# Sums of u squared of the last six chunks divided among three engines instead of two

## The chip, the core and the metric

The kernel runs on one core of one Trainium2 chip. The core has five engines that run side by side, each through its own queue in order: TensorE (PE, with PEld for its weight loads), VectorE (DVE), ScalarE (ACT), GpSimd (POOL) and SyncE (SP, which here only starts transfers). The metric is device time in microseconds. Three runs of the kernel before took 179.81, 180.15 and 180.93 us, so its median is 180.15 us.

## The reference

```python
kv = einsum('bhsd,bhse->bhde', k, v)     # per head: k^T v, 64 x 64
o  = q @ kv                            # 8 batches, 8 heads, 576 rows, 64 columns
x  = o / sqrt(mean(o*o, -1) + 1e-6) * g_norm       # then heads side by side: 4608 x 512
h  = x @ w_in                          # 4608 x 1024
e  = exp(h);   u = h * e               # softmax-weighted: solu = u / sum(e)
ln = (solu - mean(solu)) / sqrt(var(solu) + 1e-6) * g_ln
out = ln @ w_out                       # 4608 x 512
```

The kernel never forms `solu`. The factor 1/sum(e) cancels in the normalization apart from the 1e-6, so a row needs three sums over its 1024 columns: of e, of u and of u squared. They give one factor `rstd` per row, with which the product of u and the centred `w_out` is scaled.

## The kernel before

The 4608 rows are worked off in nine chunks of 512 (chunks 0 to 7 are 512 rows of a batch, chunk 8 gathers the last 64 rows of each batch). A chunk passes through: `kv_mm` (k^T v on PE, copied to `kvd`), `o_mm` (PE), `sq` (square of o, ACT), `s_mm` (mean over a head, PE), `ln` and `ex` (the root, ACT), `x` (DVE), the products with `w_in` (PE), exp (ACT), u (DVE), the turn of u, the products with `w_out` called `out` (PE), the scaling `ob` (DVE or ACT) and the `store` (SP).

Chunks 0 to 2 keep h with the 1024 columns on the partitions; their three sums are matmuls with a column of constants (`sums`), from squares `usq` and pair sums `es` that GpSimd makes. Chunks 3 to 8 (`TOK`) keep the rows on the partitions: `ht` makes 128 rows by 512 columns at a time, in eight pieces `ht.c.m.w` (m is one of four groups of 128 rows, w one of two column halves). `et` (exp) and `ut` (u) leave their row sums in `acc` by the accumulator of their instruction. The sum of u squared of a group, `st.c.m` (function `ht_sq`), is one instruction with an accumulator over 128x1024 elements, on ACT or DVE. `uT.c.y` turns u by a DMA transpose started on SP. `stats.c` (`rows_stats`, DVE) makes the variance from the 20 columns of `acc`, and `rstd.c` (ACT) its root.

The order of everything is written out ahead of time in the string `ORDER`: one entry for each piece, as `name@engine=slots`, with the engine where there is a choice and the numbers of the buffers that the piece takes (banks 0 to 7 of PSUM for matmul results, two slots `es` for the output of `st`, two slots for `u`, `acc` and others). The pieces are issued in this order, so it is the order of each engine's queue too. Whoever takes a buffer waits for its last users. Entries that matter here, with their meaning:

```
st.3.3@dve=1      sum of squares of rows 3 of chunk 3, on VectorE, output in es slot 1
ht.7.0.0=2        first product of chunk 7, into bank 2 (free when ut of the last product in it is done)
stats.5           variance of chunk 5: waits for all four st.5.m
```

Matmuls on zeros at the start (`warm`, 29 in all, their numbers in `WARM`) keep TensorE busy until data has come.

Of the kernel before, what the change touches and what calls it, by code (L numbers as in the profile page):

```python
# [20 lines left out]
warm.0=7 vf.0=00 ident kf.0=10 g q.0.0=0 v.0.1 k.0.1 q.0.1 vc.1@act q.1.0=1 vc.0@act k.1.0=1 kc.0@dve kc.1@act v.1.0=1  # L21
w_in.0 warm.1=7 qT_mm.0.0=0 w_in.1 kv_mm.0.0=1 qT.0.0@dve=0 kv.0.0.1@act kv.0.0.0@act k.1.1 kv.0.0.2@dve warm.2=7
o_mm.0.0=23 sq.0.0.0@act=00 sq.0.0.1@dve=11 warm.3=1 kv_mm.0.1=4 v.1.1 s_mm.0.0.0=5 kv.0.1.2@act turn_g=6 kv.0.1.1@dve
ex.0.0.0=0 g_mean qT_mm.0.1=7 q.1.1 s_mm.0.0.1=0 x.0.0.0=0 ex.0.0.1=1 qT.0.1@dve warm.4=5 qT_mm.1.0=1 w_out=01234567
kv.0.1.0@dve x.0.0.1 o_mm.0.1=56 sq.0.1.0@act=20 qT.1.0@dve=1 v.2.0=2 sq.0.1.1@act=31 warm.5=4 s_mm.0.1.0=2 ex.0.1.0=2
s_mm.0.1.1=0 kv_mm.1.0=7 k.2.0=2 ex.0.1.1=0 kv.1.0.2@dve table kv.1.0.1@dve kv.1.0.0@dve x.0.1.1 warm.6=2 o_mm.1.0=43
sq.1.0.1=0 x.0.1.0 warm.7=7 h_mm.0.0.0=1 sq.1.0.0=1 h_mm.0.4.0=2 s_mm.1.0.1=0 h_mm.0.2.0=7 ln.1.0.1=0 s_mm.1.0.0=6
h_mm.0.5.0=5 ln.1.0.0=1 h_mm.0.1.0=0 ex.1.0.0=1 h_mm.0.0.1 h_mm.0.7.0=6 ex.1.0.1=0 x.1.0.0=1 h_mm.0.1.1 exp.0.0=0
h_mm.0.7.1 x.1.0.1 h_mm.0.6.0=4 exp.0.1 u.0.0=0 h_mm.0.2.1 h_mm.0.6.1 usq.0.0@pool=0 u.0.1 exp.0.2=1 kv_mm.1.1=3
exp.0.6=2 u.0.2 h_mm.0.4.1 es.0.0=0 exp.0.7 kv.1.1.1@dve qT_mm.1.1=1 kv.1.1.0@dve exp.0.4=3 h_mm.0.5.1 qT.1.1@dve  # L30
# [5 lines left out]
h_mm.1.3.0=1 v.3.0=0 exp.1.6=2 h_mm.1.7.1 w_center.2 usq.0.4@pool exp.1.5 kv_mm.2.0=26 u.1.6 exp.1.7 h_mm.1.3.1
k.4.0=1 u.1.5 kv.2.0.2@act out.0.2.0=7 kv.2.0.1@act u.1.1 usq.0.7@pool kv.2.0.0@act kv.2.1.1@act qT_mm.2.0=3
w_center.7 kv.2.1.0@act kv.2.1.2@act qT_mm.2.1=2 es.1.0=1 qT.2.0@act=2 u.1.7 out.0.1.0=0 w_center.5 exp.1.3 v.4.0=1
o_mm.2.0=64 qT.2.1@dve out.0.3.0=3 sq.2.0.0=0 es.1.1 u.1.3 usq.1.0@act=1 s_mm.2.0.0=2 w_center.6 sums.0=1 ln.2.0.0=1
v.5.0=2 w_center.4 ex.2.0.0=0 es.1.3 o_mm.2.1=25 sq.2.0.1=1 turn.0 out.0.1.1 x.2.0.0=2 sq.2.1.0=2 usq.1.3@pool stats.0  # L40
out.0.3.1 sq.2.1.1=3 rstd.0 q_last.5 s_mm.2.1.0=6 s_mm.2.0.1=1 ob.0.3@dve=0 ln.2.1.0=0 out.0.2.1 usq.1.6@pool
ln.2.0.1=1 store.0.3 out.0.0.0=6 ex.2.1.0=2 usq.1.7@pool s_mm.2.1.1=3 ex.2.0.1=1 x.2.1.0 qT_mm.4.0=1 usq.1.5@pool
ln.2.1.1=0 out.0.0.1 ob.0.2@dve=3 ex.2.1.1=0 usq.1.1@pool x.2.0.1 qT_mm.3.1=2 qT_mm.3.0=3 x.2.1.1 kv_mm.3.0=74 q.7.0=2
qT.3.0@act=3 h_mm.2.0=5 usq.1.4@pool kv.3.1.1@dve qT.3.1@act ob.0.0@dve=1 h_mm.2.6=3 es.1.2 kv.3.1.0@dve ob.0.1@act=2
kv.3.0.2@dve qT.4.0@dve=0 h_mm.2.2=6 exp.2.0=0 q_last.2 kv.3.0.0@dve exp.2.6=3 u.2.0=0 h_mm.2.7=2 v.7.0=0 exp.2.2=2
u.2.6 h_mm.2.4=0 usq.1.2@pool exp.2.7 u.2.2 h_mm.2.3=1 kv.3.0.1@dve exp.2.4=1 k.5.0=2 u.2.7 h_mm.2.1=5 q_last.4
exp.2.3 u.2.4 kv.3.1.2@dve kv_mm.4.0=36 usq.2.0@pool=0 exp.2.1 u.2.3 o_mm.3.1=72 u.2.1 kv.4.1.1@act o_mm.3.0=04
es.2.0=0 sq.3.1.1=0 sums.1=1 kv.4.0.1@dve sq.3.1.0=2 kv.4.0.2@dve kv.4.1.0@dve es.2.1 sq.3.0.1=1 kv.4.1.2@dve
h_mm.2.5=5 turn.1 sq.3.0.0=3 stats.1 out.1.1.0=6 usq.2.1@pool exp.2.5 kv.4.0.0@dve usq.2.4@act s_mm.3.1.0=1 u.2.5
out.1.0.0=3 es.2.3 rstd.1 s_mm.3.0.0=5 ln.3.1.0=1 out.1.1.1 usq.2.6@pool ln.3.0.0=0 s_mm.3.1.1=1 ob.1.1@dve=7  # L50
out.1.0.1 ex.3.0.0=2 usq.2.2@pool ln.3.1.1=0 x.3.0.0=0 out.1.2.0=5 q_last.1 ex.3.1.0=1 s_mm.3.0.1=6 k.6.0=0 out.1.2.1
ex.3.1.1=0 x.3.1.0 usq.2.3@act usq.2.5@pool out.1.3.0=1 ob.1.0@dve=5 ln.3.0.1=1 x.3.1.1 store.1.0 q.6.0=1 o_mm.4.0=07
ex.3.0.1=2 ht.3.0.0=3 ob.1.2@dve=6 usq.2.7@pool sq.4.0.0=2 x.3.0.1 store.1.2 ht.3.0.1=6 et.3.0.0=00 es.2.2 ht.3.3.0=2
sq.4.0.1=3 store.0.2 et.3.0.1 v.6.0=1 out.1.3.1 et.3.3.0=2 k.7.0=1 s_mm.4.0.0=5 ob.1.3@dve=4 ht.3.2.0=4 ln.4.0.0=0
ut.3.0.0=1 ht.3.1.0=1 ex.4.0.0=1 ut.3.0.1 et.3.2.0=3 ht.3.3.1=5 x.4.0.0=1 et.3.1.0=1 ht.3.2.1=3 ut.3.2.0 st.3.0@act=1
ht.3.1.1=6 ut.3.1.0 ut.3.3.0 qT_mm.4.1=0 et.3.1.1 sums.2=4 qT.4.1@dve q.5.0=0 et.3.2.1 ut.3.1.1 q_last.7 o_mm.4.1=12
et.3.3.1 turn.2 out.2.0.0=0 q_last.3 ut.3.2.1 sq.4.1.1=0 q_last.6 out.2.1.0=6 ut.3.3.1 sq.4.1.0=1 q_last.0
st.3.1@dve=1 s_mm.4.1.1=3 s_mm.4.1.0=5 ln.4.1.1=1 out.2.0.1 stats.2 ex.4.1.1=0 out.2.3.0=3 st.3.2@dve=0 ln.4.1.0=0
out.2.2.0=4 rstd.2 x.4.1.1 ex.4.1.0=2 s_mm.4.0.1=5 out.2.2.1 st.3.3@act=1 x.4.1.0 out.2.1.1 ob.2.2@dve=0 ln.4.0.1=1
out.2.3.1 ob.2.1@dve=5 ex.4.0.1=1 ht.4.0.0=2 x.4.0.1 kv_mm.5.0=14 et.4.0.0=01 stats.3 ht.4.3.0=5 ob.2.3@dve=6  # L60
kv.5.1.1@act qT.5=1 kv.5.1.0@act ut.4.0.0=0 rstd.3 ht.4.1.0=6 et.4.3.0=1 kv.5.0.2@dve ob.2.0@dve=3 ht.4.3.1=7
et.4.1.0=3 kv.5.1.2@dve ht.4.2.0=3 ut.4.3.0 kv.5.0.0@act uT.3.0=1 et.4.3.1 ut.4.1.0 ht.4.1.1=2 et.4.2.0=2 kv.5.0.1@dve
ut.4.3.1 ht.4.0.1=0 et.4.1.1 ut.4.2.0 ht.4.2.1=4 store.2.1 et.4.0.1 ut.4.1.1 o_mm.5.1=56 et.4.2.1 ut.4.0.1 o_mm.5.0=17
kv_mm.7.0=32 sq.5.0.1=2 ut.4.2.1 uT.4.0=0 sq.5.0.0=0 s_mm.5.0.1=0 kv.7.0.1@dve kv.7.0.2@dve sq.5.1.0=1 s_mm.5.0.0=4
kv.7.0.0@dve ln.5.0.0=0 kv.7.1.2@dve out.3.1.0=3 kv.7.1.0@dve sq.5.1.1=3 kv.7.1.1@dve store.0.0 s_mm.5.1.0=4
st.4.1@dve=0 out.3.0.0=2 ex.5.0.0=0 uT.3.1 ln.5.1.0=1 out.3.1.1 x.5.0.0=2 ln.5.0.1=0 st.4.3@dve=1 out.3.0.1 ex.5.1.0=2
ex.5.0.1=1 kv_mm.6.0=41 store.2.0 x.5.1.0 st.4.2@act=0 s_mm.5.1.1=0 ob.3.0@dve=5 ht.5.0.1=5 store.2.3 x.5.0.1
ln.5.1.1=1 ht.5.0.0=2 ob.3.1@act=1 st.4.0@dve=1 store.1.1 ex.5.1.1=0 ht.5.1.0=0 et.5.0.0=10 qT.6=2 x.5.1.1 ht.5.1.1=7
kv.6.1.1@act kv.6.0.0@dve et.5.1.0=3 ut.5.0.0=1 ht.5.2.0=3 stats.4 et.5.1.1 out.3.3.0=6 uT.4.1 ut.5.1.0 et.5.2.0=0
ht.5.3.0=2 ut.5.1.1 rstd.4 out.3.3.1 kv.6.1.0@dve kv.6.0.1@dve et.5.0.1 store.1.3 ht.5.3.1=0 ob.3.3@dve=3 kv.6.0.2@act  # L70
# [731 lines left out]
```

## Time and profile before

| | before |
|---|---|
| median of three runs | 180.15 us |
| the profiled execution, its own time | 179.54 us |
| its span, first to last instruction | 177.8 us |
| PE, DVE, ACT, POOL busy | 166.1, 136.7, 145.5, 63.3 us |
| mean granted TensorE clock | 0.995 |
| transfers | 36.01 MB, mean 203 GB/s |

The span lies 1.74 us below the execution's own time; that part is ahead of the first and behind the last instruction. Busy times add up the durations of an engine's instructions; matmuls are pipelined, one shows 379 ns, but the next starts 0.216 us after it.

### The profile page before, as it was taken

The numbers are of one execution on the slowest core, as the hardware profiler recorded it, in microseconds if no ns is written. First come the engines' busy times: TensorE is split into PE (matmuls) and PEld (weight loads), VectorE is DVE, ScalarE is ACT, GpSimd is POOL, SyncE is SP. The second block draws the span as 40 slices with busy tenths as digits, with TensorE's granted clock in tenths as the row PEclk, the third lists the DMA queues.
The fourth block names the chain that finished last, engine by engine and source line by source line (L and its number), as shares of the span: only waits on it lengthen the run. The fifth ranks groups of instructions, "written<-read, shape, count | busy, mean of one in ns | idle before, by whom it ended". The sixth has DMA issues, their size and how long they took to land.

```text
span 177.8 us, 4448 instructions
## 1 busy us (share of the span) xinstructions
PE 166.1 (93%) x1725; PEld 81.6 (46%) x1746; DVE 136.7 (77%) x321; ACT 145.5 (82%) x294; POOL 63.3 (36%) x77
## 2 busy tenths in 40 slices
PE   7696999999999999999998999999999999999980
...
POOL 8754027999999999725000000000000000000000
...
GB/s 196 202 203 210 209 290 350 209 206 208 209 222 218 198 206 122 199 249 208 180 161 180 182 214 202 187 203 204 204 173 204 151 171 128 200 203 210 202 210 218
DMA packets 57737, 36.01 MB, mean 203 GB/s; under 512 B 39148, under 2 KB 51188, under 8 KB 57716
## 3 DMA queue, kind: packets, MB, share of 16 engines
...
q8 instruction: 13, 0.21, 0.5%
q14 instruction: 8, 0.07, 0.1%
...
## 4 chain that ended last, share of the span: by engine, by line
PE 82%; DVE 5%; ACT 5%; DMA 4%; issue 2%; POOL 0%; POOLq 0%
PE out_ps L685 31%; PE ht_ps L557 23%; PE h_ps L492 11%; DMA q_sb<-in_q_dram 4%; PE kv_ps L354 4%; PE s_ps L417 3%; PE o_ps L399 3%; PE sum_ps L641 2%; PE qT_ps L374 2%; ACT rst_sb L425 1%; ACT osq_sb L409 1%; DVE u_sb L507 1%; DVE kvd L189 1%; ACT lss_sb L421 1%; PE mean_ps L670 1%
## 5 line engine op out<-in xcount | busy, mean ns | idle before, releaser
L557 PE MATMUL ht_ps<-w_in_sb,x_sb 128*128 128x512 bf16 x188 | 44.0, 379 | 0.2
L685 PE MATMUL out_ps<-w_out_sb,usq_sb 128*128 128x512 bf16 x177 | 42.8, 379 | 0.5 <-DVE kvd L189 0.2
L567 ACT ACTIVATE e_sb<-ht_ps,zero_t 128x512 f32<-128x512 f32 x48 | 32.7, 685 | 5.7 <-PE ht_ps L557 5.0
L575 DVE SCALAR_TENSOR_TENSOR u_sb<-ht_ps,e_sb 128x512 bf16<-128x512 f32 x48 | 31.4, 684 | 1.0 <-ACT e_sb L567 0.7
L439 DVE SCALAR_TENSOR_TENSOR x_sb<-o_ps,g_sb,rst_sb 128x512 bf16<-128x512 f32 x36 | 26.2, 744 | 7.7 <-ACT rst_sb L425 7.5
L557 PEld LDWEIGHTS <-x_sb 128*128 128x128 bf16 x192 | 18.6, 98 | 22.4 <-DVE x_sb L439 0.2
L685 PEld LDWEIGHTS <-usq_sb 128*128 128x128 bf16 x184 | 17.7, 98 | 21.9 <-issue 1.3
L702 DVE TENSOR_SCALAR rooms<-out_ps,rstd 128x512 f32<-128x512 f32 x27 | 20.1, 748 | 8.6 <-PE out_ps L685 7.3
L409 ACT ACTIVATE osq_sb<-o_ps,zero_t 128x512 bf16<-128x512 f32 x35 | 22.1, 684 | 3.1 <-PE o_ps L399 2.9
L421 ACT ACTIVATE lss_sb<-s_ps,eps_t 128x512 f32<-128x512 f32 x32 | 21.3, 685 | 3.4 <-PE s_ps L417 3.3
L685 PE MATMUL out_ps<-w_out_sb,u_sb 128*128 128x512 bf16 x94 | 22.9, 379 | 0.2 <-issue 0.2
L492 PE MATMUL h_ps<-x_sb,w_in_sb 128*128 128x512 bf16 x91 | 22.1, 379 | 0.7 <-issue 0.3
L425 ACT ACTIVATE rst_sb<-lss_sb,zero_t 128x512 f32<-128x512 f32 x32 | 22.4, 724 | 0.4
L518 POOL TENSOR_TENSOR usq_sb<-u_sb 128x512 bf16<-128x512 bf16 x18 | 18.7, 1046 | 7.4 <-DVE u_sb L507 7.2
L586 DVE SCALAR_TENSOR_TENSOR es_sb<-u_sb 128x1024 bf16<-128x1024 bf16 x17 | 20.6, 1216 | 0.0
L500 ACT ACTIVATE e_sb<-h_ps,zero_t 128x512 f32<-128x512 f32 x24 | 15.4, 689 | 1.4 <-PE h_ps L492 1.3
L507 DVE TENSOR_TENSOR u_sb<-h_ps,e_sb 128x512 bf16<-128x512 f32 x24 | 15.5, 682 | 0.5 <-ACT e_sb L500 0.4
L524 POOL TENSOR_TENSOR es_sb<-e_sb 128x512 bf16<-128x512 f32 x12 | 15.3, 1275 | 1.2 <-ACT e_sb L500 1.1
L685 PEld LDWEIGHTS <-u_sb 128*128 128x128 bf16 x96 | 9.0, 98 | 10.8 <-issue 0.6
L417 PE MATMUL s_ps<-osq_sb,head_mean 128*128 128x512 bf16 x36 | 13.0, 379 | 1.0 <-ACT osq_sb L409 0.9
L492 PEld LDWEIGHTS <-w_in_sb 128*128 128x128 bf16 x96 | 8.8, 98 | 10.7 <-issue 1.1
L189 DVE CAST kvd<-kv_ps 64x128 bf16<-64x128 f32 (+1 forms) x31 | 8.9, 287 | 3.2 <-PE kv_ps L354 2.2
...
## 6 DMA issues: line engine op xcount, KB each, us to landing
out_dram<-rooms SPq DMA_DIRECT2D x66, 128.0 KB, 2.5
...
q_sb<-in_q_dram POOLq DMA_DIRECT2D x6, 512.0 KB, 10.4
...
```

Source lines behind the costliest of these rows:

```text
L409: nc.scalar.activation(out=t[:, :], in_=o, func=AF.Square, bias=zero_t[:, :])
L421: nc.scalar.activation(out=t[:, :], in_=T["s", i][:, :], func=AF.Ln, bias=eps_t[:, :])
L425: nc.scalar.activation(out=t.rearrange("p a b c -> p (a b c)"), in_=T["lss", i][:, :], func=AF.Exp, scale=-0.5, bias=zero_t[:, :])
L439: nc.vector.scalar_tensor_tensor(out=dst, in0=T["o", c, hf, z][:, :, :, :], scalar=g_rep[:, :], in1=T["rst", (c, hf, z)][:, :, :, :], op0= ...
L492: nc.tensor.matmul(T["h", c, f][:, :], w_in_sb[:, dt, f * 128:(f + 1) * 128], T["x", c][:, dt, :], start=(dt == 0), stop=(dt == NP - 1),)
L518: of(engine).tensor_tensor(out=dst, in0=src, in1=src, op=MUL)
L557: nc.tensor.matmul(t[:, :], T["x", c][:, dt, 128 * m:128 * m + 128], w_in_sb[:, dt, 512 * w:512 * w + 512], start=(dt == 0), stop=(dt == N ...
L567: nc.scalar.activation(out=T["e", c, m][:, w, :], in_=T["ht", c, m, w][:, :], func=AF.Exp, bias=zero_t[:, :], accum_out=T["acc", c][:, 2 * ...
L575: nc.vector.scalar_tensor_tensor(out=T["u", c][:, m, 512 * w:512 * w + 512], in0=T["ht", c, m, w][:, :], scalar=1.0, in1=T["e", c, m][:, w ...
L586: nc.vector.scalar_tensor_tensor(out=t, in0=u, scalar=1.0, in1=u, op0=MUL, op1=MUL, accum_out=total)
L685: nc.tensor.matmul(T["out", c, m][:, :], u_rows(c, f, m), w_out_sb[:, f, :], start=(f == 0), stop=(f == NF - 1),)
L702: nc.vector.tensor_scalar_mul(out=dst, in0=src, scalar1=by)
```

## The change

For chunks 3 to 8 `st` gets a third engine to choose from, GpSimd. There a sum is not one instruction but eleven: the product u times u into an fp32 tile of 128x1024, then ten additions of the right half to the left half (512, 256, ... 1 columns), the last of them into the column of `acc`.

```diff
     def ht_sq(engine, c, m):
+        u, total = T["u", c][:, m, :], T["acc", c][:, 16 + m:17 + m]
+        if engine == "pool":
+            t = tile_of(("es", c, m), [128, d_ff], FP32)
+            nc.gpsimd.tensor_tensor(out=t[:, :], in0=u, in1=u, op=MUL)
+            w = d_ff // 2
+            while w:
+                dst = t[:, 0:w] if w > 1 else total
+                nc.gpsimd.tensor_tensor(out=dst, in0=t[:, 0:w], in1=t[:, w:2 * w], op=ADD)
+                w //= 2
+            return
         t = tile_of(("es", c, m), [128, 2, d_ff], BF16)[:, 0, :]
-        u, total = T["u", c][:, m, :], T["acc", c][:, 16 + m:17 + m]
...
-            plan.add(("st", c, m), "act|dve", lambda e, c=c, m=m: ht_sq(e, c, m), ...
+            plan.add(("st", c, m), "act|dve|pool", lambda e, c=c, m=m: ht_sq(e, c, m), ...
...
-    WARM = (12, 4, 3, 2, 1, 2, 3, 2)
+    WARM = (12, 4, 6, 7)
```

The whole table `ORDER` is another one. It holds the same pieces (but the 29 warm matmuls stand in four groups instead of eight) in another order and partly on other engines. The 24 sums of squares go from 17 on DVE and 7 on ACT to 9 on DVE, 1 on ACT and 14 on POOL:

```diff
-st.3.0@act=1 st.3.1@dve=1 st.3.2@dve=0 st.3.3@act=1 st.4.1@dve=0 st.4.3@dve=1 st.4.2@act=0 st.4.0@dve=1
-st.5.2@dve=0 st.5.1@dve=1 st.5.3@dve=0 st.5.0@dve=1 st.6.1@dve=0 st.6.3@dve=1 st.6.2@act=0 st.7.0@dve=1
-st.6.0@dve=0 st.7.1@dve=1 st.7.3@dve=0 st.7.2@dve=1 st.8.0@act=0 st.8.2@dve=1 st.8.1@act=0 st.8.3@act=1
+st.3.0@pool=1 st.3.2@dve=0 st.3.1@pool=0 st.4.0@pool=1 st.4.2@pool=0 st.3.3@dve=1 st.4.3@pool=1 st.5.0@pool=0
+st.4.1@dve=1 st.5.1@pool=0 st.5.2@pool=1 st.5.3@pool=0 st.6.0@dve=1 st.6.1@pool=0 st.6.2@pool=1 st.6.3@act=0
+st.7.1@dve=1 st.7.2@pool=0 st.7.3@dve=1 st.7.0@dve=1 st.8.0@pool=0 st.8.1@dve=1 st.8.3@pool=1 st.8.2@dve=0
```

The stretch of the new table around `stats.5`, in full:

```
...
out.5.3.0=4 et.6.3.0=3 x.7.1.0 ht.6.1.1=2 sq.7.0.1=3 ut.6.3.0 out.5.0.1 et.6.1.1 stats.5
s_mm.7.1.1=3 out.5.3.1 ut.6.1.1 ln.7.1.1=0 st.6.0@dve=1 st.6.1@pool=0 uT.6.0=0 s_mm.7.0.1=0 ht.7.0.0=2 ln.7.0.1=1
...
```

And around the third `o_mm`:

```
...
kv_mm.1.0=4 x.0.0.1 ex.0.1.0=1 kv.1.0.1@dve table kv.1.0.2@dve x.0.1.0 x.0.1.1 kv.1.0.0@act warm.3=7 o_mm.1.0=52 h_mm.0.2.0=7
...
```

More of the change, by code (lines that the diff above doesn't have):

```diff
@@ L20 @@
 ORDER = """
[L21 to L30, printed above, removed]
@@ L36 @@
[L36 to L45, printed above, removed]
@@ L46 @@
[L46 to L70, printed above, removed]
@@ L96 @@
-store.8.0@sp store.8.1@act ob.8.3.1@dve store.8.2@act store.8.3.1@sp
+warm.0=7 vf.0=00 ident kf.0=10 g q.0.0=0 v.0.1 k.0.1 q.0.1 vc.0@dve q.1.0=1 vc.1@dve k.1.0=1 kc.1@act kc.0@dve v.1.0=1
+w_in.0 warm.1=7 qT_mm.0.0=0 w_in.1 kv_mm.0.0=1 kv.0.0.1@dve kv.0.0.2@dve v.1.1 kv.0.0.0@dve qT.0.0@dve=0 warm.2=7
+o_mm.0.0=23 turn_g=4 sq.0.0.0@dve=00 sq.0.0.1@act=11 k.1.1 kv_mm.0.1=5 s_mm.0.0.1=6 kv.0.1.2@act g_mean qT_mm.0.1=7
+q.1.1 kv.0.1.1@dve qT.0.1@dve kv.0.1.0@act ex.0.0.1=0 w_out=01234567 o_mm.0.1=10 s_mm.0.0.0=4 sq.0.1.1@act=21
```

104 lines of the change are left out of this document (73 added, 31 removed).

## The prediction, on record before the changed kernel ran

> **What bounds the kernel now.** I read the page first (span, busy time, slices), then the busy time by stretch, then the chain that ended last.
>
> ```profile
> span 177.8 us, 4448 instructions
> ...
> PE 166.1 (93%) x1725; PEld 81.6 (46%) x1746; DVE 136.7 (77%) x321; ACT 145.5 (82%) x294; POOL 63.3 (36%) x77
> ...
> PE   7696999999999999999998999999999999999980
> ...
> POOL 8754027999999999725000000000000000000000
> ```
>
> ```profile
> 70.00:95.00 25.00, 24.84 (x272) 12.23 (x276) 20.96 (x57) 22.27 (x54) 7.97 (x10) 1.00 1.23 196
> 95.00:128.00 33.00, 32.05 (x321) 15.14 (x321) 30.82 (x71) 31.57 (x67) 0.00 (x0) 1.00 1.00 196
> 128.00:162.00 34.00, 33.79 (x215) 15.57 (x218) 31.50 (x78) 27.72 (x65) 0.00 (x0) 1.00 0.85 178
> 162.00:178.00 16.00, 10.74 (x57) 5.48 (x56) 4.79 (x16) 6.66 (x13) 0.00 (x0) 0.93 0.82 208
> ```
>
> ```profile
> PE 82%; DVE 5%; ACT 5%; DMA 4%; issue 2%; POOL 0%; POOLq 0%
> ```
>
> In the stretches the columns behind the length are busy PE, PEld, DVE, ACT and POOL, then the granted clock. PE is the bound: from 70 to 162 us it is idle for 0.16 + 0.95 + 0.21 = 1.3 us at full clock, and it holds 82% of the chain. DVE and ACT follow closely (30.8 and 31.6 of 33 us between 95 and 128). POOL, empty from about 82 us on, is on the chain nowhere. So relieving DVE and ACT can give back 1.3 us here at most, while a wait that reaches PE costs its full length.
>
> **What a sum costs on GpSimd.** It takes 14 of the 24 sums over. On the engines that lose them a sum is one instruction of 1.2 us:
>
> ```profile
> L586 DVE SCALAR_TENSOR_TENSOR es_sb<-u_sb 128x1024 bf16<-128x1024 bf16 x17 | 20.6, 1216 | 0.0
> ...
> L584 ACT ACTIVATE es_sb<-u_sb,zero_t 128x1024 bf16<-128x1024 bf16 x7 | 8.0, 1142 | 0.0
> ```
>
> DVE is rid of 8 x 1.22 = 9.8 us, ACT of 6 x 1.14 = 6.8 us; both are hidden behind PE, so this is worth the idle time named above and no more. On POOL it is eleven instructions, each of which waits for the one before to be complete. No row has the fp32 addition in place; the nearest are these (duration and mean of one behind the bar; in the second fence start, duration):
>
> ```profile
> L518 POOL TENSOR_TENSOR usq_sb<-u_sb 128x512 bf16<-128x512 bf16 x18 | 18.7, 1046 | 7.4 <-DVE u_sb L507 7.2
> ...
> L524 POOL TENSOR_TENSOR es_sb<-e_sb 128x512 bf16<-128x512 f32 x12 | 15.3, 1275 | 1.2 <-ACT e_sb L500 1.1
> ```
>
> ```profile
> 0.74 0.20 POOL masks.py:197 MEMSET ident<- 128x128 bf16 x1 [0.29 <-POOLq L786]
> 1.02 0.29 POOL masks.py:199 TENSOR_SCALAR_AFFINE_SELECT ident<-ident 128x128 bf16<-128x128 bf16 x1
> 1.27 0.10 POOL masks.py:197 MEMSET eye<- 9x9 f32 x1
> 1.44 0.19 POOL masks.py:199 TENSOR_SCALAR_AFFINE_SELECT eye<-eye 9x9 f32<-9x9 f32 x1
> ...
> 78.28 0.74 POOL L278 DMA_DIRECT2D q_sb<-in_q_dram  x1 [4.01 <-PE qT_ps L374]
> 79.47 2.97 POOL L302 DMA_DIRECT2D q_last<-in_q_dram  x4 [0.45 <-issue]
> ```
>
> The tiny write of 9 elements shows 0.10 us, and the select that needs it starts 0.17 us after it: a fixed 0.10 and 0.07 to the next dependent one. With that, fp32 costs (1275 - 100) / 512 = 2.29 ns an element and bf16 (1046 - 100) / 512 = 1.85. The product: 1024 x 1.85 ns + 0.10 + 0.07 = 2.06 us. The additions run over 1023 elements in all: 1023 x 2.29 ns = 2.34 us, and 10 x 0.17 = 1.7 us fixed, 4.04. One sum: 6.1 us, which I take, since these rows are an fp32 operand and a dependent pair. With the additions at the bf16 rate it is 1.89 + 1.7 + 2.06 = 5.6. With the 0.19 us of the small select as fixed part, 2.12 and 1.67 ns an element follow, and 2.6 + 2.17 + 1.97 = 6.7; with the product at that fp32 rate too, 7.2. Below stands 4.2: 2047 elements at 1046 / 512 = 2.04 ns and nothing fixed. 14 x 6.1 = 85 us fit into the rest of the run; what matters is when each must be done.
>
> The GPSIMD Engine Reference of the Trainium skill, section 3.1, gives 4497 ns for an fp32 addition of 2048 elements, 2.2 ns an element against 2.29 here; by that estimate the sum would be 0.1 us shorter, 6.0, and the forecast 0.7 us lower.
>
> **When it must be done.** The new table puts st.3.0 on POOL behind the load q.5.0 and three q_last. By the last two rows above, with three of four (0.74 each), POOL is free at 78.28 + 0.74 + 0.45 + 2.2 = 81.7. Between st.3.0 and st.4.0 PE has 48 matmuls of 512 columns and two `kv_mm`; between st.4.0 and stats.5 it has 19 `out` and 16 `ht` groups of 4 and 10 `s_mm`, 150 matmuls, one `kv_mm` and six `o_mm`. Prices, from the chain in order of time and the timeline (start, length):
>
> ```profile
> 88.08 0.71 PE kv_ps L354 x72
> ...
> 143.85 5.18 PE ht_ps L557 x24
> ```
>
> ```profile
> 94.86 0.63 PE L399 MATMUL o_ps<-qT_sb,kvd 64*64 64x256 bf16 x16
> ```
>
> 5.18 / 24 = 0.216 a matmul. First stretch: 10.4 + 1.4 = 11.8 us, so st.4.0 falls due at 93.5. Second: 32.4 + 0.7 + 1.9 = 35.0, with half of the 0.95 us of idle time of that stage 35.5; stats.5 stands at 129.0 and reaches its third instruction at 129.4:
>
> ```profile
> 128.17 0.16 DVE L599 TENSOR_REDUCE two<-acc_sb 128x8 f32<-128x16 f32 x1
> ...
> 128.57 0.16 DVE L605 SCALAR_TENSOR_TENSOR var<-sq,acc_sb 128x4 f32<-128x4 f32 x1
> ```
>
> That is the first one that reads the sums of squares, so there DVE waits for st.5.3. Between the two places POOL's queue holds seven sums in a row: st.4.0, 4.2, 4.3, 5.0, 5.1, 5.2, 5.3. They fit if one takes (129.4 - 93.5) / 7 = 5.13 us or less. At 6.1 the two sums before end at 81.7 + 12.2 = 93.9, and the seven at 93.9 + 42.7 = 136.6: 7.2 us late. Behind the waiting instruction stands ut.6.1.1; it frees bank 2, which ht.7.0.0 needs, and PE has only six matmuls (1.3 us, what DVE needs for the rest of stats.5 and ut.6.1.1) before it. So PE stands still for about the 7.2 us. The earlier waits of DVE, st.3.3 for st.4.0's slot and st.4.1 for st.4.3's, are parts of the same lateness and not added. After stats.5 the remaining five sums lie 6 to 13 us apart, and st.8.3 has `out` groups behind it to the end; I add nothing.
>
> **The start.** In the new table the copy kv.1.0.0, which the third `o_mm` needs, is on ACT behind the table load:
>
> ```profile
> 18.24 1.28 ACT L445 ACT_TABLE_LOAD   x1
> ...
> 19.17 0.41 PE L399 MATMUL o_ps<-qT_sb,kvd 64*64 64x256 bf16 x8 [0.24 <-DVE kvd L189]
> ```
>
> ```profile
> L187 ACT CAST kvd<-kv_ps 64x128 bf16<-64x128 f32 (+1 forms) x17 | 4.3, 261 | 3.8 <-PE kv_ps L354 3.6
> ```
>
> 18.24 + 1.28 + 0.26 for a copy, and 0.05 to pass on, is 19.8 instead of 19.17: 0.7 us later, at a place where PE has only warm matmuls (bounds: 0, if the table load comes early enough, to 1.3, its whole length). The remaining moves of loads, copies and scalings have the same counts and I price them at nothing; the cover is PE's own work, and if it is gone, each costs a copy of 0.3 or a scaling of 0.7 us. The load queue keeps its transfers.
>
> **The sum**, against the profiled execution's 179.54 us (the median is 180.15): + 7.2 for the wait at stats.5, + 0.7 at the start, - 0.95 for idle PE time between 95 and 128 that lighter DVE and ACT give back. That is 186.5 us.
>
> **The rivals.**
>
> *GpSimd is in time.* If a sum takes up to 5.13 us, nothing waits: 179.54 + 0.7 - 0.95 = 179.3, no change. For it: the lower bound of 4.2, and four independent squares in 4.04 us on POOL, so that fixed parts can overlap. Against it: here each step needs the one before.
>
> *Faster.* GpSimd is in time, the start is not later, PE's 1.3 us of idle time vanish, and the last store lands sooner. It is issued at 173.34 and the span ends 4.5 us later, where stores take 2.5 us at the median:
>
> ```profile
> out_dram<-rooms SPq DMA_DIRECT2D x66, 128.0 KB, 2.5
> ```
>
> ```profile
> 173.34 0.33 SPq L715 DMA_DIRECT2D out_dram<-rooms  x1
> ```
>
> With 1 us of these 2, 179.54 - 1.3 - 1.0 = 177.2. It decides as soon as a sum is below 5.13 us. Against it: the tail's stores are as many as before, and PE's work is the same.
>
> *VectorE and GpSimd hold each other up.* The nine sums left on DVE read u from SBUF twice while POOL is reading too. If one had to stand until the other's instruction is over, DVE would lose up to 2.06 us at each, about 9 us at half; it has 33 - 30.82 + 34 - 31.5 = 4.7 us free and gains 9.8, so most is hidden. But POOL would lose 1.22 us to each of the two DVE sums inside its chain (st.3.3, st.4.1): with 5.13 us a sum, 179.3 + 2.4 and some 0.8 on PE for unhidden waits, 182.5; on top of the forecast, 188.9. No run here shows such a pair: POOL's last arithmetic ends at 72.8 and DVE's first sum comes later.
>
> ```profile
> 71.51 1.27 POOL L524 TENSOR_TENSOR es_sb<-e_sb 128x512 bf16<-128x512 f32 x1
> ```
>
> The page SBUF — State Buffer of the Trainium skill, section "Who interferes with whom", states this rule: a DVE instruction with two SBUF inputs contends with a GpSimd instruction that reads SBUF, and the second fully blocks.
>
> **How the numbers follow.** Chances: the wait at stats.5 0.55, the holding up alone 0.07 (slower together 0.62), in time 0.22 (no change), faster 0.16. A measurement of this kernel can tell about 1% from no change, 178.3 to 182.0. The forecast's own range: at 5.6 us a sum the chain ends at 93.5 + 39.2 = 132.7, 3.3 late, 182.6; at 6.7 it ends at 95.1 + 46.9 = 142.0, 12.6 late, 191.9 (at 7.2 it would be 196.4). The whole range goes from 178.5, which takes in most of the case without change, to 192.
>
> **What would show it.** In the profile after: POOL's steps with some 6.1 us from one product to the next between 94 and 137 us and no gap; a wait of DVE at the variance of chunk 5, for POOL, of about 7 us, the longest of the run; directly behind it a hole in PE ahead of an `ht` matmul. Waits of DVE for POOL also ahead of st.3.3. The third `o_mm` near 19.8. The forecast is wrong if products follow each other at 5.1 us or less, or if DVE waits and PE does not.

## The result, and the profile after

The changed kernel took 203.07 us at the median (201.56 to 205.79, six runs) beside 179.98 us of the kernel before: ratio 1.1243 [1.1176, 1.131]. Two of the six runs lie more than 1.5% above the fastest and are left out of the ratio. The kernel is slower, as predicted, but by some 22 us instead of the 7.0 of the prediction's sum, and outside the predicted range. The profiled execution took 201.56 us, 22.0 more than that of before. The page first:

```profile
span 199.8 us, 4610 instructions
...
PE 172.1 (86%) x1746; PEld 82.7 (41%) x1746; DVE 136.3 (68%) x304; ACT 138.7 (69%) x282; POOL 154.8 (77%) x232
...
PE   7868999999999999999934999998069998999930
...
POOL 8751089999799994989889988988877989178910
PEclk9999999999999999999995899999657999999996
...
POOL 42%; PE 34%; issue 6%; DMA 5%; ACT 5%; DVE 3%; ACTq 0%; POOLq 0%; DVEq 0%
```

POOL, empty from 82 us on before, is busy in nearly every slice behind that, and it now holds 42% of the chain that ended last. PE has two notches, and a lower clock behind each. Busy time by stretch (columns as before):

```profile
95.00:128.00 33.00, 26.52 (x209) 11.66 (x208) 22.87 (x53) 23.88 (x51) 29.24 (x53) 0.90 0.87 166
128.00:162.00 34.00, 26.50 (x124) 11.14 (x121) 19.31 (x47) 21.49 (x49) 28.32 (x55) 0.85 0.62 122
```

PE idles 6.5 and 7.5 us where it idled 0.95 and 0.21. What a sum costs stands in the groups of POOL by shape (busy time and mean of one, then the idle time ahead of all of them):

```profile
L585 POOL TENSOR_TENSOR es_sb<-u_sb 128x1024 f32<-128x1024 bf16 x14 | 28.1, 2008 | 7.2 <-DVE u_sb L576 6.8 <-ACT es_sb L594 0.4
L589 POOL TENSOR_TENSOR es_sb<-es_sb 128x512 f32<-128x512 f32 x14 | 20.3, 1454 | 1.1
...
L589 POOL TENSOR_TENSOR es_sb<-es_sb 128x2 f32<-128x2 f32 x14 | 2.7, 194 | 1.1
L589 POOL TENSOR_TENSOR acc_sb<-es_sb 128x1 f32<-128x1 f32 x14 | 2.7, 193 | 1.1
```

and the products in the timeline of POOL (start, length), the first of the run and four in a row:

```profile
82.56 1.94 POOL L585 TENSOR_TENSOR es_sb<-u_sb 128x1024 f32<-128x1024 bf16 x1
...
117.63 1.89 POOL L585 TENSOR_TENSOR es_sb<-u_sb 128x1024 f32<-128x1024 bf16 x1
...
125.29 1.89 POOL L585 TENSOR_TENSOR es_sb<-u_sb 128x1024 f32<-128x1024 bf16 x1
...
131.95 1.89 POOL L585 TENSOR_TENSOR es_sb<-u_sb 128x1024 f32<-128x1024 bf16 x1
...
138.61 1.89 POOL L585 TENSOR_TENSOR es_sb<-u_sb 128x1024 f32<-128x1024 bf16 x1
```

From product to product it is 6.66 us (131.95 to 138.61), or 7.66 (117.63 to 125.29) where something comes between. An addition of one or two columns takes 0.19 us and 0.08 pass to the next one (1.1 us over 14). Now the ends of this, in the timelines of DVE and PE (the wait and its releaser in brackets):

```profile
103.54 2.89 DVE L596 SCALAR_TENSOR_TENSOR es_sb<-u_sb 128x1024 bf16<-128x1024 bf16 x1 [5.43 <-POOL acc_sb L589]
...
145.34 0.16 DVE L615 SCALAR_TENSOR_TENSOR var<-sq,acc_sb 128x4 f32<-128x4 f32 x1 [8.30 <-POOL acc_sb L589]
...
191.06 0.16 DVE L615 SCALAR_TENSOR_TENSOR var<-sq,acc_sb 128x4 f32<-128x4 f32 x1 [2.67 <-POOL acc_sb L589]
```

```profile
107.16 0.61 PE L418 MATMUL s_ps<-osq_sb,head_mean 128*128 128x512 bf16 x1 [5.72 <-DVE x_sb L440]
...
146.36 3.57 PE L558 MATMUL ht_ps<-w_in_sb,x_sb 128*128 128x512 bf16 x8 [7.50 <-DVE u_sb L576]
...
190.70 1.04 PE L704 MATMUL acc_ps<-w_out_sb,usq_sb 128*128 128x256 bf16 x8
```

st.3.3 waits 5.43 us and PE stands 5.72 us behind it; the variance of chunk 5 waits 8.30 us and PE stands 7.50 us, ahead of ht.7.0.0. The last matmuls of before, for comparison:

```profile
171.75 1.04 PE L694 MATMUL acc_ps<-w_out_sb,usq_sb 128*128 128x256 bf16 x8
```

So the 22.0 us between the two spans fall into three parts: 145.34 - 128.57 = 16.8 us up to the variance of chunk 5; from there to PE's end 46.4 us instead of 44.2, 2.2 more; and behind PE's end 8.1 us instead of 5.0, 3.1 more.

One thing more is seen in DVE's groups. The nine sums left there last 1784 ns on average instead of 1216; the one at 103.54 above lasts 2.89 us:

```profile
L596 DVE SCALAR_TENSOR_TENSOR es_sb<-u_sb 128x1024 bf16<-128x1024 bf16 x9 | 16.1, 1784 | 5.5 <-POOL acc_sb L589 5.4
```

### The profile page after: what moved, and what is told of

Same layout as the page of the kernel before. It is cut to its first block, busy times and chain, and to the rows that moved or that the text cites. A ratio compares the mean times of both kernels' runs of the same rounds, so it can differ in the third digit from the quotient of the medians.

```text
span 199.8 us, 4610 instructions
## 1 busy us (share of the span) xinstructions
PE 172.1 (86%) x1746; PEld 82.7 (41%) x1746; DVE 136.3 (68%) x304; ACT 138.7 (69%) x282; POOL 154.8 (77%) x232
## 4 chain that ended last, share of the span: by engine, by line
POOL 42%; PE 34%; issue 6%; DMA 5%; ACT 5%; DVE 3%; ACTq 0%; POOLq 0%; DVEq 0%
POOL es_sb L589 26%; POOL es_sb L585 11%; PE h_ps L493 10%; PE out_ps L695 9%; PE ht_ps L558 7%; DMA v_sb<-in_v_dram 5%; PE sum_ps L651 2%; PE s_ps L418 2%; DVE u_sb L576 2%; POOL q_sb L279 2%; PE kv_ps L355 1%; ACT e_sb L501 1%; PE qT_ps L375 1%; POOL acc_sb L589 1%; PE mean_ps L680 1%
## 5 line engine op out<-in xcount | busy, mean ns | idle before, releaser
L589 POOL TENSOR_TENSOR es_sb<-es_sb 128x512 f32<-128x512 f32 (+8 forms) x126 | 59.8, 475 | 9.9
L558 PE MATMUL ht_ps<-w_in_sb,x_sb 128*128 128x512 bf16 x192 | 47.3, 399 | 8.0 <-DVE u_sb L576 7.5
L695 PE MATMUL out_ps<-w_out_sb,usq_sb 128*128 128x512 bf16 x184 | 44.7, 385 | 0.6 <-ACT lss_sb L422 0.6
L568 ACT ACTIVATE e_sb<-ht_ps,zero_t 128x512 f32<-128x512 f32 x48 | 32.7, 685 | 17.2 <-PE ht_ps L558 16.8
L585 POOL TENSOR_TENSOR es_sb<-u_sb 128x1024 f32<-128x1024 bf16 x14 | 28.1, 2008 | 7.2 <-DVE u_sb L576 6.8
L558 PEld LDWEIGHTS <-x_sb 128*128 128x128 bf16 x192 | 19.3, 102 | 33.3 <-issue 12.9
L695 PE MATMUL out_ps<-w_out_sb,u_sb 128*128 128x512 bf16 x96 | 23.7, 379 | 0.0
L525 POOL TENSOR_TENSOR es_sb<-e_sb 128x512 bf16<-128x512 f32 x12 | 15.3, 1278 | 9.8 <-ACT e_sb L501 9.8
L493 PE MATMUL h_ps<-x_sb,w_in_sb 128*128 128x512 bf16 x96 | 22.8, 379 | 0.0
L596 DVE SCALAR_TENSOR_TENSOR es_sb<-u_sb 128x1024 bf16<-128x1024 bf16 x9 | 16.1, 1784 | 5.5 <-POOL acc_sb L589 5.4
L418 PE MATMUL s_ps<-osq_sb,head_mean 128*128 128x512 bf16 x36 | 13.6, 385 | 7.2 <-DVE x_sb L440 5.7
L519 POOL TENSOR_TENSOR usq_sb<-u_sb 128x512 bf16<-128x512 bf16 x19 | 19.6, 1046 | 0.1
L508 DVE TENSOR_TENSOR u_sb<-h_ps,e_sb 128x512 bf16<-128x512 f32 x24 | 15.3, 681 | 1.3 <-ACT e_sb L501 1.1
```

The costliest lines, as they stand in the source:

```text
L493: nc.tensor.matmul(T["h", c, f][:, :], w_in_sb[:, dt, f * 128:(f + 1) * 128], T["x", c][:, dt, :], start=(dt == 0), stop=(dt == NP - 1),)
L558: nc.tensor.matmul(t[:, :], T["x", c][:, dt, 128 * m:128 * m + 128], w_in_sb[:, dt, 512 * w:512 * w + 512], start=(dt == 0), stop=(dt == N ...
L568: nc.scalar.activation(out=T["e", c, m][:, w, :], in_=T["ht", c, m, w][:, :], func=AF.Exp, bias=zero_t[:, :], accum_out=T["acc", c][:, 2 * ...
L585: nc.gpsimd.tensor_tensor(out=t[:, :], in0=u, in1=u, op=MUL)
L589: nc.gpsimd.tensor_tensor(out=dst, in0=t[:, 0:w], in1=t[:, w:2 * w], op=ADD)
L695: nc.tensor.matmul(T["out", c, m][:, :], u_rows(c, f, m), w_out_sb[:, f, :], start=(f == 0), stop=(f == NF - 1),)
```

## The experiments

All are the changed kernel with the edit shown, e9 apart, which is the kernel before. The kernel before ran beside each and took 179.6 to 180.1 us.

**How much is the length of a sum.** e1 keeps of each GpSimd sum the product and one addition, e2 six of the eleven steps (so both leave part of the sum out), and e4 gives GpSimd's sums to ACT and DVE.

```diff
-            w = d_ff // 2
-            while w: ...            # product, 512, 256, ..., 1
+            # e1: product, one column + constant
+            # e2: product, 512, 256, 128, 64, one column + constant
+            # e4: ORDER, the 14 st.c.m@pool -> 8 @act, 6 @dve, in the same places
```

> The changed kernel with the same order table, but a sum on GpSimd is two instructions instead of eleven: the product, and one addition of one column (a constant is added there; the additions of 512 to 2 columns are left out). By the rows of the changed kernel that is 1.97 + 0.26 = 2.2 us instead of 6.66. Theory of the late chain: the nine sums that GpSimd does in a row end long before the variance of chunk 5 asks for them, no wait of VectorE for GpSimd is left, and the time is 179.3 us (178 to 181). Rival, the table itself (its order, or VectorE and GpSimd holding each other up at SBUF) costs the time: 185 us or more.

> As the kernel with two steps, but six: the product, the additions of 512, 256, 128 and 64 columns, and the one of a single column with a constant (those of 32 to 2 are left out): 1.97 + 1.35 + 0.81 + 0.54 + 0.39 + 0.26 = 5.3 us. Theory of the late chain: there is a point (about 4.8 us plain, with 0.85 us more at some four collisions) up to which nothing is lost. Nine sums from 82.6 us end at 82.6 + 47.7 + 3.4 = 133.7, 4.3 us after the 129.4 at which the variance of chunk 5 could start: 184 to 187 us with what follows. Rival, time lost in proportion to GpSimd's work, without such a point: 179.3 + 23.7 * (5.3 - 2.2) / (6.66 - 2.2) = 195.8 us.

> The changed kernel's table with the 14 sums of GpSimd given back to ScalarE (8) and VectorE (6), one instruction each, in the same places. It shows what the other moves of the table are worth. Theory of the late chain: without GpSimd's sums the table is as good as the one before, 179 to 181.5 us. Rival, the table by itself is worse (start, copies, scalings): 184 us or more.

| run | plain step from product to product | us | ratio |
|---|---|---|---|
| e1 | 2.13 us | 183.42 | 1.0204 [1.0134, 1.0275] |
| e2 | 5.20 us | 185.62 | 1.0308 [1.024, 1.0377] |
| changed kernel | 6.66 us | 203.07 | 1.1243 [1.1176, 1.131] |
| e4 | none on GpSimd | 187.47 | 1.044 [1.0352, 1.0528] |

The waits of DVE for POOL in e2 (total, times, longest):

```profile
DVE var L615 <- POOL acc_sb L590: 1.2, 1, 1.2
...
DVE es_sb L596 <- POOL acc_sb L590: 1.0, 1, 1.0
```

3 us more in a sum cost 2 us in all, the next 1.5 us cost some 17: there is a threshold, and 5.2 us is near it. Beyond it most of it comes through (17 of 14 x 1.46 = 20 us). e1 shows where the table itself has its place for the variance of chunk 5, since DVE waits for no sum there:

```profile
132.73 0.16 DVE L615 SCALAR_TENSOR_TENSOR var<-sq,acc_sb 128x4 f32<-128x4 f32 x1
```

That is 3.3 us behind the 129.4 of the prediction, in an execution whose first product came at 83.78. The table, with no sum that is late, lies 3.6 us above the kernel before that ran beside it, which is neither the 178 to 181 us of the theory nor the 185 of the rival; with none on GpSimd it lies 7.6 above. So in this table the relief of DVE and ACT is worth 4 us (e4 against e1), and yet e1 is not faster than the kernel before.

**Are the waits one lateness?** e5 takes away what st.3.3 waits for; e6 fills the two holes of PE with warm matmuls, so that the clock has no reason to fall.

```diff
-        "es": 2,    ... st.3.3@dve=1
+        "es": 3,    ... st.3.3@dve=2                                  # e5
-    WARM = (12, 4, 6, 7)            ... s_mm.5.0.1=4 ...  ht.7.0.0=2
+    WARM = (12, 4, 6, 7, 22, 30)    ... warm.4=7 s_mm.5.0.1=4 ... warm.5=3 ht.7.0.0=2   # e6
```

> The changed kernel with a third output slot, which st.3.3 takes, so that VectorE no longer waits for st.4.0 ahead of it (5.4 us in the changed kernel's trace, and TensorE stood 5.7 us behind it). The prediction held that the two waits are parts of one lateness. Theory of the late chain: GpSimd's chain ends as before at some 145 us, the wait at the variance of chunk 5 grows by about what the first one loses, and the time falls by a clock dip at most: 200.5 to 203 us. Rival, the waits add up: 203 - 5.5 = 197.5 us.

e5 took 203.09 us, 1.1311 [1.125, 1.1372]. In its timeline of DVE the wait has moved to the next sum, st.4.1, while the one at the variance stays nearly as long as it was (7.76 instead of 8.30):

```profile
119.43 2.89 DVE L596 SCALAR_TENSOR_TENSOR es_sb<-u_sb 128x1024 bf16<-128x1024 bf16 x1 [5.14 <-POOL acc_sb L589]
...
147.06 0.16 DVE L615 SCALAR_TENSOR_TENSOR var<-sq,acc_sb 128x4 f32<-128x4 f32 x1 [7.76 <-POOL acc_sb L589]
```

The first product came 1.7 us later than in the changed kernel's profile (84.27), and so did the variance. The end of POOL's chain is what counts; where DVE waits for it on the way made no difference to the time.

> The changed kernel with matmuls on zeros put into TensorE's two holes: 22 (4.7 us) ahead of the s_mm of chunk 5 that waits for x, 30 (6.5 us) ahead of ht.7.0.0, in banks that are free there. They change no wait. In the changed kernel the granted clock fell to 0.50 in the five microseconds after each hole. Theory: the dip costs some 2 to 3 us at the two places beyond the waits themselves: 200 to 201.5 us, with a granted clock near 1.00 from 100 to 160 us. Rival, the dip costs nothing because DVE is the slower one there: 203 us.

e6 took 203.81 us, 1.1349 [1.1281, 1.1417]. The clock in 105 to 110 us is 1.00 there, but only 0.50 in the changed kernel (first row e6, second the changed kernel), and it buys nothing:

```profile
105.00:110.00 5.00, 4.05 (x19) 1.66 (x17) 4.83 (x11) 0.69 (x1) 4.69 (x5) 1.00 1.06 209
```

```profile
105.00:110.00 5.00, 2.36 (x6) 0.77 (x7) 4.80 (x11) 1.31 (x4) 4.45 (x8) 0.50 1.01 200
```

What PE saves DVE spends in e6 at the next wait for POOL:

```profile
161.52 2.89 DVE L596 SCALAR_TENSOR_TENSOR es_sb<-u_sb 128x1024 bf16<-128x1024 bf16 x1 [2.49 <-POOL acc_sb L589]
```

Here the fallen clock beside a late queue cost no time of its own; I had thought it would.

**Do DVE and GpSimd hold each other up?** e7 gives DVE's nine sums to ACT, e3 lets DVE finish GpSimd's sums, e12 leaves every other sum on GpSimd.

```diff
+   e7:  st.3.2 3.3 4.1 6.0 7.0 7.1 7.3 8.1 8.2   @dve -> @act
+   e3:  GpSimd: product, 512, 256 columns; DVE: tensor_reduce of 128x256 ahead of the variance
+   e12: st.3.1 4.2 6.1 @pool -> @dve; st.5.0 5.2 8.0 8.3 @pool -> @act
```

> The changed kernel with the nine sums of VectorE given to ScalarE in the same places, so that no sum of VectorE reads SBUF twice while GpSimd reads. In the changed kernel three of the nine sums in the chain took 7.4 to 7.6 us instead of 6.66, and VectorE's sums 1.78 us instead of 1.22. Theory of the two holding each other up: all of GpSimd's sums take 6.66, the chain ends at 82.6 + 9 * 6.66 = 142.5 instead of 145.3, the two last sums end 1.7 us earlier: 198 to 200 us. Rival, the longer steps have another cause: 7.5 us sums stay, 203 us.

e7 took 197.67 us, 1.1002 [1.0945, 1.1059]: by the two ratios some 4.3 us less than the changed kernel, although ACT has nine sums more. The nine sums of GpSimd up to the variance of chunk 5 follow at 6.66 to 6.8 us, and the variance comes 1.3 us sooner although the first product starts 1.2 us later:

```profile
144.03 0.16 DVE L615 SCALAR_TENSOR_TENSOR var<-sq,acc_sb 128x4 f32<-128x4 f32 x1 [4.82 <-POOL acc_sb L589]
```

The chain up to there is 2.5 us shorter. The edit also moves the waits for a slot from DVE to ACT, and what that is worth is not told apart in the time. The groups of DVE in e7 show which small operations still meet GpSimd:

```profile
L615 DVE SCALAR_TENSOR_TENSOR var<-sq,acc_sb 128x4 f32<-128x4 f32 x6 | 3.8, 627 | 8.0 <-POOL acc_sb L589 6.4 <-ACT es_sb L594 1.2
L613 DVE TENSOR_TENSOR sq<-two 128x8 f32<-128x8 f32 x6 | 3.5, 581 | 0.2
L609 DVE TENSOR_REDUCE two<-acc_sb 128x8 f32<-128x16 f32 x6 | 1.0, 162 | 0.0
```

The two with two SBUF inputs average 0.6 us, the reduce with one is 0.16 as before. In e1 one can be seen singly, between POOL's product and the next (DVE, then POOL):

```profile
114.68 1.88 DVE L613 TENSOR_TENSOR sq<-two 128x8 f32<-128x8 f32 x1
...
116.79 1.89 DVE L619 SCALAR_TENSOR_TENSOR vare<-sq,var 128x4 f32<-128x4 f32 x1
```

```profile
114.64 1.89 POOL L587 TENSOR_TENSOR es_sb<-u_sb 128x1024 f32<-128x1024 bf16 x1 [1.41 <-DVE two L609]
...
116.77 1.89 POOL L587 TENSOR_TENSOR es_sb<-u_sb 128x1024 f32<-128x1024 bf16 x1
```

An operation on 128x8 that takes 0.17 us alone lasts as long as the product that started 0.04 us before it, and ends 0.03 us after it. The Trainium skill states in SBUF — State Buffer, "Who interferes with whom", that a DVE instruction with two SBUF inputs contends with a GpSimd instruction that reads SBUF, that what they share is an exclusive lock, and that the order of issue decides which one blocks; the trace agrees, with 1.88 us beside 1.89.

> The changed kernel's table; GpSimd makes the product and the additions of 512 and 256 columns, and leaves 256 columns per sum that VectorE reduces (one TENSOR_REDUCE of 128x256 for each) just ahead of the variance. Everything is computed. GpSimd 1.97 + 1.35 + 0.81 = 4.1 us a sum, VectorE 14 times some 0.33 us. Theory of the late chain: nine sums end at 82.6 + 37.2 + 3.4 = 123.2 us, in time; TensorE stays the bound and the relief of VectorE and ScalarE is worth 1.3 us at most: 178.5 to 180.5 us. Rival, the relief is worth more because both engines are nearly full: 176 to 177.5 us.

e3 took 191.20 us, 1.0612 [1.0543, 1.0682]. No long wait for POOL is left, but DVE pays (its groups):

```profile
L597 DVE SCALAR_TENSOR_TENSOR es_sb<-u_sb 128x1024 bf16<-128x1024 bf16 x9 | 14.9, 1659 | 0.1
L610 DVE TENSOR_REDUCE acc_sb<-part 128x1 f32<-128x256 f32 x14 | 5.1, 410 | 0.0
L624 DVE SCALAR_TENSOR_TENSOR vare<-sq,var 128x4 f32<-128x4 f32 x6 | 4.5, 755 | 0.2
L618 DVE TENSOR_TENSOR sq<-two 128x8 f32<-128x8 f32 x6 | 4.2, 700 | 0.2
```

At some 4 us a sum it should lie between e1 and e2, if only lateness counted; it lies 5.6 us above e2, and above both ranges of its expectation. That the longer and added instructions of DVE are the cause is read from these groups and not tested apart.

> The changed table with seven of the fourteen sums left on GpSimd (st.3.0, 4.0, 4.3, 5.1, 5.3, 6.2, 7.2), the other seven in the same places on ACT (5.0, 5.2, 8.0, 8.3) and DVE (3.1, 4.2, 6.1); everything is computed. Places of the table are then 10 us apart and more for sums of 6.7 to 7.6 us, so GpSimd is in time. My theory: lateness alone makes the changed kernel slow, so this lies at the level of the table with very short sums, 183.4, up to 185.5 (DVE sums still collide with GpSimd). The rival: the holding up of DVE and GpSimd costs by itself, in time or not: 187 to 191, at or above the 187.5 of the table with no sum on GpSimd. Both exclude a time below 180.

e12 took 188.89 us, 1.052 [1.0433, 1.0608]: the rival's side. With half of the sums GpSimd is nearly in time (DVE waits 2.1 us for it in all), and still the time is not below that without GpSimd (187.47; the intervals of e12 and e4 overlap). Its twelve sums on DVE last 1547 ns:

```profile
L596 DVE SCALAR_TENSOR_TENSOR es_sb<-u_sb 128x1024 bf16<-128x1024 bf16 x12 | 18.5, 1547 | 2.2 <-POOL acc_sb L589 2.1
```

18.5 us in all; the fifteen that e4 leaves on DVE take 18.1, undisturbed:

```profile
L596 DVE SCALAR_TENSOR_TENSOR es_sb<-u_sb 128x1024 bf16<-128x1024 bf16 x15 | 18.1, 1220 | 0.1
```

DVE has won nothing from three sums less.

**The tail.** e10 puts the last two sums on ACT.

```diff
-st.8.0@pool=0 ... st.8.3@pool=1
+st.8.0@act=0 ... st.8.3@act=1
```

> The changed kernel with the last two sums of chunk 8, st.8.0 and st.8.3, on ACT instead of GpSimd; everything is computed. My theory: the sums behind stats.5, which the prediction put at nothing, set the end too: st.8.3 on GpSimd ends at 191.0 us and the statistics of chunk 8 wait 2.67 us for it. With both on ACT the last wait for GpSimd is gone, and the time falls by the 2.7 us and up to 2 more: 198 to 200.5 us. The rival: the end follows from the 16 us lost by the middle of the run alone, PE and the stores are what is left there, and the time stays at 202.5 to 203.5.

e10 took 202.63 us (200.53 to 203.07), 1.124 [1.1152, 1.1327]: not to be told from 203.07. In its timeline the variance of chunk 8 waits for nothing and PE ends as follows:

```profile
191.41 0.16 DVE L615 SCALAR_TENSOR_TENSOR var<-sq,acc_sb 128x4 f32<-128x4 f32 x1
...
194.40 1.04 PE L704 MATMUL acc_ps<-w_out_sb,usq_sb 128*128 128x256 bf16 x8
```

Behind PE's end (195.44) there are 5.4 us of span (5.0 in the kernel before) instead of 8.1. So the trace shows 2.7 us less behind PE's end. But this execution's first product came 3.0 us later (85.57), and the median does not show the gain.

**What is left of the table.** e9 is the kernel before with three sums on GpSimd and a third buffer; the others look for the 3.6 us of e1. e13 to e16 fill the hole of PE ahead of the second `o_mm`, in which the kernel before had a warm matmul and a turn of q.

```diff
+   e9:  kernel before, "es": 3, st.5.2@pool=2 st.6.1@pool=2 st.7.0@pool=2
+   e8:  e1 and sq, var, vare as 12 tensor_scalar operations on one column, each with one SBUF tensor
+   e11: e1 and the nine sums of DVE on ACT
+   e13: e1,  e14: e8,  e15: e12,  e16: the changed kernel, each with
-    WARM = (12, 4, 6, 7)        ... o_mm.0.1=10
+    WARM = (12, 4, 6, 7, 7)     ... warm.4=0 o_mm.0.1=10
```

> The kernel before with its own table, three of its DVE sums (st.5.2, st.6.1, st.7.0) on GpSimd in the new way and a third buffer for the product; everything is computed. No place is due within 12 us of the one before. My theory: PE is the bound before (1.3 us idle between 70 and 162), so relief of DVE is worth little, and each GpSimd sum meets one or two DVE sums that it holds up: 180 to 182.5 us. The rival: relief in time is worth the idle PE time, 178 to 179.

e9 took 179.89 us, 1.001 [0.9972, 1.0048]: no change, and between the two sides' ranges (180 to 182.5 and 178 to 179), nearer to the theory's. PE's idle time falls to 0.70 and 0.03 us (0.95 and 0.21 before):

```profile
95.00:128.00 33.00, 32.30 (x326) 15.23 (x326) 29.82 (x69) 31.50 (x68) 6.80 (x11) 1.00 1.01 198
128.00:162.00 34.00, 33.97 (x219) 15.46 (x218) 31.13 (x74) 27.86 (x66) 13.63 (x22) 1.00 0.91 186
```

That is 0.43 us, below what can be measured, though each of the three sums takes 7.6 us. Where the sums have time they cost nothing that can be measured, and there is next to nothing to win.

> The kernel with two steps per GpSimd sum (the additions of 512 to 2 columns left out), and the small operations of the variance in another form: twelve of one column each with one tensor and its factors as scalars per row, instead of three with two tensors from SBUF. In the two-step kernel `sq` took 773 ns on average and `vare` 449 instead of 167 and 162, up to 1.9 us, the length of GpSimd's product. Theory: VectorE waits in them until GpSimd's instruction is over; without the second tensor they are short, and of the 3.3 us that the two-step kernel still loses some 2 to 3 are gone: 180 to 181.5 us. Rival, these were long for another reason, or the loss is the table's order: 183.5 us or more, since there are more instructions.

> The changed table with the very short GpSimd sums (product and one addition of a constant in one column, the additions of 512 to 2 columns left out) and the nine sums of DVE on ACT, so that no DVE sum meets a GpSimd instruction. With DVE's sums there it took 183.42 us. My theory: the 3.4 us over the kernel before are of two kinds, collisions and the table's own order with its later start; without the collisions 181 to 182.5. The rival: the order alone costs it, or ACT becomes the bound: 183.4 or more.

e8 took 184.46 us, 1.024 [1.0169, 1.031], and e11 186.21, 1.0374 [1.0294, 1.0455]: neither gains on e1's 183.42. In e11 ACT takes over as bound (147.6 us busy, and DVE waits 25.4 us for `rst`, 15.3 in e1).

> The table with very short GpSimd sums (product and one addition of a constant in one column, the additions of 512 to 2 columns left out; 183.42 us so far), with seven warm matmuls more in the hole of PE ahead of the second o_mm. My theory: the hole of 1.74 us there is what lets the granted clock fall to 0.50 in the next 2 us and shifts all behind it by 1 to 1.5 us (third o_mm at 20.61 instead of 19.17): the clock stays at 1.00, the third o_mm stands near 19.4, and the time is 181.5 to 182.7. The rival: a late start is hidden again by later waits (for loads, or for DVE and ACT), and the time stays at 183.2 to 183.8.

> The same with the statistics of chunks 3 to 8 in twelve column operations with one SBUF tensor input each, which GpSimd doesn't hold up. My theory: with equal starts, the small two-input operations that last 1.9 us during a product are what makes PE idle 1.3 us longer between 95 and 128 us than in the kernel before: 0.5 to 1.3 us less than the run with two-input statistics beside it. The rival: the twelve operations cost what they save, equal within 0.4 us.

e13 took 183.78 us, 1.0199 [1.0133, 1.0265], e14 184.25, 1.0207 [1.0147, 1.0267]. In e1 the hole and what follows look like this in the timeline of PE and the 2 us behind it:

```profile
14.78 0.64 PE L402 MATMUL o_ps<-qT_sb,kvd 64*64 64x256 bf16 x8 [1.74 <-DVE qT_sb L190]
...
20.61 0.41 PE L402 MATMUL o_ps<-qT_sb,kvd 64*64 64x256 bf16 x8 [0.32 <-ACT kvd L188]
```

```profile
15.00:17.00 2.00, 2.00 (x18) 1.14 (x11) 0.15 (x1) 1.53 (x3) 0.75 (x1) 0.50 1.17 209
```

In e13 the clock of the same stretch is 1.00, yet the third `o_mm` comes only 0.46 us sooner, and the time does not fall:

```profile
20.15 0.41 PE L402 MATMUL o_ps<-qT_sb,kvd 64*64 64x256 bf16 x8
```

```profile
95.00:128.00 33.00, 30.66 (x245) 14.01 (x247) 27.96 (x62) 28.29 (x61) 14.30 (x14) 1.00 1.02 198
128.00:162.00 34.00, 33.65 (x214) 15.46 (x216) 28.40 (x67) 28.98 (x67) 9.70 (x7) 1.00 0.88 171
```

In e14 PE idles only 0.69 us instead of 2.34 between 95 and 128, so in these two executions the small operations make that hole; but 1.28 us of it come back in the next stretch:

```profile
95.00:128.00 33.00, 32.31 (x252) 14.52 (x254) 28.18 (x81) 30.39 (x65) 14.02 (x14) 1.00 0.97 192
128.00:162.00 34.00, 32.37 (x207) 14.76 (x211) 29.68 (x82) 27.30 (x63) 10.59 (x8) 1.00 0.90 179
```

> Seven of the fourteen sums on GpSimd, the other seven on ACT (four) and DVE (three), all computed (188.89 us so far, third o_mm at 21.45), with the seven warm matmuls in the hole ahead of the second o_mm. My theory: 1.5 to 2.3 us less, 186.6 to 187.5. The rival: DVE and ACT set its pace later in any case, and it stays at 188.5 to 189.3.

> The changed kernel, all computed, with the seven warm matmuls in the hole ahead of the second o_mm. GpSimd's first sum waits for chunk 3's u, so a start that is earlier moves the whole chain of sums. My theory: 0.5 to 1.5 us less than the changed kernel's median of 203.07, 201.5 to 202.5. The rival: GpSimd's chain hangs on its last load and not on the start, and the time stays at 203.

e15 took 187.93 us, 1.0418 [1.0348, 1.0488], and e16 203.12, 1.1255 [1.1176, 1.1335]. e15 lies 1 us under e12, between what the two sides expected, and the intervals of the two overlap; e16 gains nothing. None of the sixteen kernels is faster than the kernel before.

## Why the prediction was right or wrong

**Right: the mechanism.** GpSimd's chain is late at the variance of chunk 5, DVE waits there longest (8.30 us), PE stands directly behind it ahead of an `ht` matmul (7.50), and at 5.20 us a sum next to nothing waits (e2: 1.2 and 1.0 us; the prediction's limit was 5.13). That st.3.3's wait is a part of the same lateness, not to be added, e5 shows.

**Wrong: the price of a sum, 6.1 us.** It was 6.66 without disturbance. The product came out as forecast (1.89 + 0.08 against 2.06). The error is in the fixed part of the ten dependent steps, 0.17 us as put, 0.19 + 0.08 = 0.27 as measured: ten times 0.10 is 1.0 us, of which the cheaper product and a smaller price per element give a part back. The write of nine elements was the wrong row for it; the small select with 0.19 us, from which the upper value of 6.7 was worked out, was the right one, and its prices per element fit too (2.12 and 1.67 ns; without disturbance 512 columns took 1.27 us and the product 1.89, so 2.11 and 1.66). With nine sums it is 9 x 0.56 = 5.0 us. Since nine sums stand in the chain, a price of 6.0 would have put the forecast 0.9 us lower, not 0.7.

**Wrong: the holding up, counted for nothing in the forecast.** Three of those nine sums took 7.51 to 7.66 us, 2.8 us in all. Together with a chain that began 0.9 us later (82.56 instead of 81.7), the nine ended at 145.3 instead of 136.6: 15.9 us behind the due time of 129.4, not 7.2. The rival had the mechanism and 2.4 us for it (1.22 at two sums of DVE; it was 0.85 to 1.0 at three, st.3.2 as well), but with a chance of 0.07. Giving DVE's sums to ACT (e7) is worth some 4.3 us.

**Wrong: nothing behind stats.5, and no cost in the tail.** It was 2.2 us up to PE's end and 3.1 behind it. Behind the hole eight `ht` matmuls took 3.57 us instead of 8 x 0.216 = 1.7, at a fallen clock; but in e6, where the clock stays up, the same time goes to the next wait for POOL. The prediction had the five sums there 6 to 13 us apart and so in time; at 6.66 us and more each, three of them (products at 146.45, 154.30 and 161.41 in the changed kernel) leave POOL idle for only 0.3 to 0.4 us between them. st.8.3 ended at 191.0, when PE's last matmuls were running; e10's trace gives 2.7 us for the two last sums.

**Wrong: the table priced at the start alone.** Without lateness (e1, e13) it is 3.6 to 3.7 us slower than the kernel before beside it, where the prediction had 0.7 of start and 0.95 of gain. The third `o_mm`, forecast near 19.8, came at 19.34 in the changed kernel's profiled execution, and between 19.9 and 22.0 in those with edits that lie behind it. In e13's execution (183.99, 4.45 us above that of before) the third `o_mm` is 1.0 us later, PE idles 1.6 us more between 70 and 162 us (0.26 + 2.34 + 0.35 against 1.32), and from PE's end to the span's it takes 1.0 us more. Filling the early hole (e13) or removing the held-up operations (e14) moved these pieces without bringing the time down; what in the order makes up the rest stays open. The gain of 0.95 us was not seen: e9, which has three sums' relief without the table, gets 0.43.

Up to stats.5 the account is closed, since POOL's nine sums follow each other without a gap: their start, length and collisions give the 145.3. The 5.3 us behind it are measured, and only in part explained. With 6.7 us a sum, which gave 191.9, and with the 2.8 us of collisions, the 0.9 of the later chain, the 0.95 not gained and the 5.3 put in afterwards, the prediction's sum comes to 201.9 beside 201.56. That is bookkeeping and no test, and in part luck: the 0.7 for the start stands in it, while the third `o_mm` of that execution came only 0.17 us later.
